# w2's gradient computed transposed, with the hidden activations as the moving side

## The chip, the cores and the metric

The kernel runs on one core of one Trainium2 chip. The metric is the device time of one execution in microseconds. A core has five engines that work side by side and wait for each other through semaphores: PE (matmuls), DVE (elementwise work and reductions), ACT (activations and copies), POOL, and SP, which here only issues transfers. SP, ACT and POOL each issue DMA transfers into a queue of their own; a transfer can be a plain copy or a DMA transpose of 2-byte elements. A matmul takes a stationary side (`lhsT`, 128 rows by up to 128 columns, loaded by a separate weight load) and a moving side (`rhs`, up to 512 columns here) and adds into PSUM, which has eight banks of 512 fp32 columns per partition.

## What is computed

One transformer block (a pre-LayerNorm linear attention with 32 heads, then a pre-LayerNorm SwiGLU MLP), forward and backward, in bf16: S = 2048 rows, D = 640, F = 1728.

```python
x = A_x
h = x + _A_ref(_layernorm(x), A_wqkv, A_wo)
h2 = h + _B_ref(_layernorm(h), B_w1, B_w3, B_w2)

def _B_ref(x, w1, w3, w2):
    gate = x @ w1                    # (2048, 640) @ (640, 1728)
    up = x @ w3
    h = silu(gate) * up              # called hh in the kernel
    return h @ w2                    # (2048, 1728) @ (1728, 640)

_out, _vjp = jax.vjp(_f, A_x, A_wqkv, A_wo, B_w1, B_w3, B_w2)
_grads = _vjp(grad_out)              # out_1 .. out_6
```

(The four matmuls are written here with `@`; the reference has them as einsums.) `out_6` is the gradient of w2: `hh.T @ grad_out`, 1728 rows by 640 columns, a sum over the 2048 rows of the sequence. It is the output that the change is about.

## The kernel before

All of it is one program, written out engine by engine in program order; each engine works its own instructions in that order. The stages, with their times in the profile:

- LayerNorm 1, the projections, the attention's sums (to about 107 us), and then attention output, LayerNorm 2 and the whole MLP forward with the elementwise half of its backward (to 341.8 us). It leaves `hh` transposed in DRAM as `hh_d` [F, S], and the gradients of gate and up as `gg_d` [2F, S].
- The w2 gradient (L1026 to L1096; 341.8 to 400.7 us), called *gw* here after its PSUM tile.
- The attention backward's first loop (L1242 to L1276; 400.7 to about 537 us), over the 16 tiles of 128 rows, `t` = 0 to 15.
- The rest of the attention backward (to 700.8 us), and at the end the gradients of w1 and w3 (L1538 to L1547; 700.8 to 817.4 us).

**gw before.** `load_hh(b)` brings a block of `hh_d` into SBUF by DMA transpose on SP's queue, as `hb[b]` [128, 16 row tiles, columns of F]. The blocks `blk` start at 0, 512, 1024 and 1536; the first is brought in two pieces of 256 columns so that PE can start on the first piece. `grad_out` lies in SBUF as `g2` [128, 16, 640]. For each 128 columns of F (`fc`, 13 of them) PE takes `hb` as the stationary and `g2` as the moving side, in two halves of 320 columns (`HD`), over 16 row tiles: 32 matmuls into two PSUM banks. ACT copies the two banks out (L1085) as one [128, 640] tile and stores it straight to `out_6` (L1086). The last 64 columns of F are `gw2_tail`: 32 matmuls of 64 stationary columns, the two halves of D in two halves of the array. While this runs, SP also loads what the next loop needs: w1 and w3 transposed (`load_w13`, into `w13a`, `w13b`) and the first two blocks of `gg_d` (`load_gg`, tiles `ggb`, two buffers, 256 rows of S each).

**The attention backward's first loop.** For tile t, PE does `ghn` (`b_ghn`, 54 matmuls of 320 columns: the gradient that comes back through the MLP to LayerNorm 2). ACT reads its PSUM tile (`gs`, L1139), DVE makes `wb`, ACT makes `y` (L1151) and DVE adds it into `g_h[:, t, :]`, the gradient of h (L1152). `b_gT(t)` then turns that tile on its side with a DMA transpose **on ACT's queue** (`ghT`, L1164, two buffers) for t < 14; the last two are turned on PE. PE uses it in `b_gr(t)` (`gr`, L1184, 10 matmuls), which stands in program order inside `b_ghn(t + 2)`, after four of its six groups of nine matmuls. DVE then makes `g_q[:, t, :]` from gr, the row tile `r_sb[:, t, :]` and others. Behind `ghT` on ACT's queue stands one more small DMA transpose for t = 1 to 10 (`woT`, then `kvN`, L1264), and at every even t from 2 on the second half of a `ggb` block (L1266). SP issues the first half of that `ggb` block, then `hnb` and `r_sb` for tile t + 2 (`b_load`), and from t = 4 on a tile of `xn_d` (`load_xn`), in this order; `hnb` has three buffers and so waits until `wb` of tile t - 1 is done.

**Order and waits.** Each transfer from SP or ACT counts up one of eight semaphores, given out in turn, and the builder lets a transfer wait until the one before it on the same semaphore has landed, so that eight are in flight at most. It adds waits for the data and, for DMA transposes, waits on transposes of the other queue. A waiting instruction holds everything behind it on its engine.

**The end.** The last loop (L1538) makes 35 products of up to 496 columns (`job`, `grad_job`), copies each out by ACT and stores it from ACT's queue; the first six are stored in two halves each.

Of the kernel before, what the change touches and what calls it, by code (L numbers as in the profile page):

```python
# [9 lines left out]
P = 128  # L10
BF16 = mybir.dt.bfloat16
F32 = mybir.dt.float32
# [6 lines left out]
S, D, H, F = 2048, 640, 32, 1728  # L19
DH = D // H  # L20
ST, DT = S // P, D // P
FT, FP = 14, 1792
FL = F - 13 * P
W, SC, TPC = 512, 4, 4
HD = D // 2
NG = 27
# [29 lines left out]
def kernel(  # L56
# [19 lines left out]
    V, A, T, G, SY = nc.vector, nc.scalar, nc.tensor, nc.gpsimd, nc.sync  # L76
    dma, dmaT, dmaG = SY.dma_start, SY.dma_start_transpose, G.dma_start
# [12 lines left out]
    dram = ctx.enter_context(tc.tile_pool(name="dram", bufs=1, space=bass.MemoryType.DRAM))  # L90
# [5 lines left out]
    w_d = dram.tile([D, D], BF16, name="w_d")  # L96
    kvT_d = dram.tile([D, D], BF16, name="kvT_d")
    dwoT_d = dram.tile([D, D], BF16, name="dwoT_d")
    hn_d = dram.tile([S, D], BF16, name="hn_d")
    hh_d = dram.tile([F, S], BF16, name="hh_d")  # L100
    gg_d = dram.tile([2 * F, S], BF16, name="gg_d")
# [2 lines left out]
    def pool(name, side="left", space=None):  # L104
        kw = dict(space=space) if space is not None else dict(side=side)
        return tc.alloc_tile_pool(name=name, bufs=1, reuse_waits="tile", **kw)
# [71 lines left out]
    ps = pool("p1p", space=PSUM)  # L178
# [48 lines left out]
    def load_w13(c0, c1):  # L227
        def go1():
            dma(out=w1[:, c0:c1, 0:F], in_=rows(B_w1)[:, c0:c1, :])

        def go3():
            dma(out=w3[:, c0:c1, :], in_=rows(B_w3)[:, c0:c1, 0:F - FL])
        return [go1, go3]
# [18 lines left out]
    def p1_tr(t, parts=((0, DT),)):  # L252
        xn = x_sb[:, t, :]
        for a, b in parts:
            tr = ps.tile([P, DT, P], BF16, name="tr", bufs=2)
            for c in range(a, b):
                T.transpose(tr[:, c, :], xn[:, c * P:(c + 1) * P], ident[:])

            A.copy(out=pqT[:, a:b, t * P:(t + 1) * P], in_=tr[:, a:b, :])  # L259
# [13 lines left out]
    def p1_mm(t, n0, between=None, halves=None):  # L273
        acc = p1_acc() if halves is None else None
        for j in range(2):
            p1_half(acc[:, j, 0:HD] if halves is None else halves[j][:, 0:HD], t, n0 + j * HD)
            if j == 0 and between is not None:
                between()
        return acc
# [241 lines left out]
    for t in range(ST):  # L521
        first = None
        if t < RAW:
# [11 lines left out]
            k = p1_mm(t, D, between, kh)  # L535
            act(0, 1)
            act(1, 1)
        else:
            k = p1_mm(t, D, (lambda: p1_tr(t + 1)) if t + 1 < XT_DMA else None)
# [95 lines left out]
    ps = pool("pap", space=PSUM)  # L635
# [342 lines left out]
    for c in range(SC):  # L978
# [9 lines left out]
        for fc in range(FT):  # L988
# [8 lines left out]
            if c == 0 and fc in (5, 7, 9, 11):  # L997
                a, b = {5: (0, 3), 7: (3, 6), 9: (6, 10), 11: (10, 13)}[fc]
# [10 lines left out]
            if c == SC - 1 and fc == 0:  # L1009
                g2 = U1.tile([P, ST, D], BF16, name="g2", tag="Q")  # L1010
                tail = U2.tile([P, DT, P], BF16, name="w13tail", tag="g2T", bufs=2)
            if c == SC - 1 and fc in (1, 2, 5, 6):
                i = (1, 2, 5, 6).index(fc)
# [9 lines left out]
    drain(1)  # L1023


    hb, blk = {}, [(0, 512), (512, 512), (1024, 512), (1536, 192)]  # L1026

    def load_hh(b):
        f0, fw = blk[b]
        hb[b] = U2.tile([P, ST, 512], BF16, name="hb", tag="ABCA"[b])  # L1030
        for a, n in ((0, 2 * P), (2 * P, 2 * P)) if b == 0 else ((0, fw),):
            dmaT(out=hb[b][:, :, a:a + n], in_=hh_d[f0 + a:f0 + a + n, :])

    load_hh(0)
    for _ in o2_steps(SC - 1, A.dma_start):
# [7 lines left out]
    br = pool("br", "right")  # L1043
    ps = pool("pcp", space=PSUM)
# [12 lines left out]
    def load_gg(j, c0, c1, q=dma):  # L1057
        if c0 == 0:
            ggb[j] = ba.tile([P, NG, 2 * P], BF16, name="ggb", bufs=2)
        q(out=ggb[j][:, c0:c1, :],  # L1060
            in_=gg_d[c0 * P:c1 * P, j * 2 * P:(j + 1) * 2 * P].rearrange("(c p) w -> p c w", p=P))

    def gw2_tail():

        gt = ps.tile([P, 2, 512], F32, name="gt", tag="gw", bufs=4)
        for t in range(ST):
            for j in range(2):
                T.matmul(gt[j * FL:(j + 1) * FL, 0, 0:HD], lhsT=hb[3][:, t, P:P + FL],
                         rhs=g2[:, t, j * HD:(j + 1) * HD], start=(t == 0), stop=(t == ST - 1))
        ob = br.tile([P, HD], BF16, name="gts")  # L1070
        A.copy(out=ob[:], in_=gt[:, 0, 0:HD])
        for j in range(2):
            A.dma_start(out=out_6[F - FL:F, j * HD:(j + 1) * HD], in_=ob[j * FL:(j + 1) * FL, :])

    for fc in range(FT - 1):
        b, i = divmod(fc, 4)
        if fc == FT - 2:
            gw2_tail()
        acc = ps.tile([P, 2, 512], F32, name="gw", bufs=4)
        for j in range(2):  # L1080
            for t in range(ST):
                T.matmul(acc[:, j, 0:HD], lhsT=hb[b][:, t, i * P:(i + 1) * P], rhs=g2[:, t, j * HD:(j + 1) * HD],  # L1082
                         start=(t == 0), stop=(t == ST - 1))
        ob = br.tile([P, D], BF16, name="gw2o", bufs=2)
        A.copy(out=ob[:].rearrange("p (j n) -> p j n", j=2), in_=acc[:, :, 0:HD])  # L1085
        A.dma_start(out=out_6[fc * P:(fc + 1) * P, :], in_=ob[:])  # L1086
        if fc == 3:
            load_hh(3)
        if fc == 5:
            load_w13()  # L1090
        if fc == 8:
            load_gg(0, 0, NG)
        if fc == 11:
            load_gg(1, 0, NG)
    ps.release()
    U2.release()  # L1096

# [6 lines left out]
    g_q = bl.tile([P, ST, D], BF16, name="g_q")  # L1104
    bo = pool("bo")
    r_sb = bo.tile([P, ST, D], BF16, name="r_sb")
    ps = pool("pbp", space=PSUM)
# [6 lines left out]
    def b_load(t):  # L1114
        hnb[t] = br.tile([P, D], BF16, name="hnb", bufs=3)
        dma(out=hnb[t][:], in_=hn_v[:, t, :])
        dma(out=r_sb[:, t, :], in_=r_v[:, t, :])
# [40 lines left out]
    def by_dma(t):  # L1158
        return t < ST - 2
# [35 lines left out]
    def b_gq(t):  # L1195
        V.tensor_tensor(out=two(sz[t][:]), in0=gr.pop(t)[:, :, 0:HD], in1=two(sz[t][:]), op=ALU.add)
        V.tensor_tensor(out=g_q[:, t, :], in0=sz.pop(t)[:], in1=cc.pop(t)[:], op=ALU.mult)
# [30 lines left out]
    def load_xn(a, b):  # L1228
        dma(out=xnN[:, a:b, :], in_=xn_v[:, a:b, :])
# [3 lines left out]
    def load_xnT(c):  # L1233
# [3 lines left out]
            xnT[c], xnT[c + 1] = both[:, 0], both[:, 1]  # L1237
        dmaT(out=xnT[c], in_=xn_d[c * W:(c + 1) * W, :])

    b_load(0)  # L1240
    b_load(1)
    for t in range(ST):  # L1242
        g = b_ghn(t)

        def part():
            next(g, None)

        u = t - 2
        ahead = 2 <= t <= ST - 4 and t % 2 == 0
        if ahead:  # L1250
            load_gg(t // 2 + 1, 0, FT)
        part()
        part()
        part()
        if t + 2 < ST:
            b_load(t + 2)
        if t >= 1:
            ln_rest.pop(t - 1)()
            if by_dma(t - 1):
                b_gT(t - 1)  # L1260
            if t <= 2 * DT:
                n = (t - 1) % DT
                dst, src = (woT, A_wo) if t <= DT else (kvN, kvT_d)
                A.dma_start_transpose(out=dst[:, :, n * P:(n + 1) * P], in_=src[n * P:(n + 1) * P, :])  # L1264
            if ahead:
                load_gg(t // 2 + 1, FT, NG, A.dma_start)  # L1266
        part()
        if u >= 0:
            b_gr(u)
        part()  # L1270
        part()
        if u >= 0:
            b_gq(u)

        if t >= 4:
            load_xn(t - 4, t - 3)  # L1276


    tri = U1.tile([P, 2 * DT, D], BF16, name="tri", tag="S0")
# [7 lines left out]
    a, b = ST - 1, ST - 2  # L1287
# [66 lines left out]
    ps = pool("pdp", space=PSUM)  # L1354
# [3 lines left out]
    def d_acc():  # L1358
        return ps.tile([P, 2, 512], F32, name="dkv", bufs=3)
# [20 lines left out]
    for m, (a, b) in enumerate(M_H):  # L1380
        n = (b - a) * DH
        acc = ps.tile([P, 512], F32, name="gkvT", tag="dkv", bufs=3)
        for c in range(DT):
            T.matmul(acc[:, 0:n], lhsT=woT[:, c, m * P:(m + 1) * P], rhs=QT[:, c, a * DH:b * DH], start=(c == 0),
                     stop=(c == DT - 1))
# [38 lines left out]
    acc = d_acc()  # L1424
    for m in range(DT):
        T.matmul(acc[:, m // 4, m % 4 * P:(m % 4 + 1) * P], lhsT=ones[:], rhs=gzd[:, m, :], start=(m % 4 == 0),
                 stop=True, skip_group_check=True)
# [3 lines left out]
    for t in range(ST):  # L1431
        c, i = divmod(t, TPC)
        u = t // 2
        acc = d_acc()
        for j in range(2):
            for k in range(DT):
                T.matmul(acc[:, j, 0:HD], lhsT=xnT[c][:, k, i * P:(i + 1) * P], rhs=gm[:, k, j * HD:(j + 1) * HD],  # L1437
                         start=(k == 0), stop=(k == DT - 1))
# [7 lines left out]
        if t in (2, 5, 8, 11, 14):  # L1446
            n = t // 3
            acc = square(mN, gkv_b, n)
            k = (4, 0, 1, 2, 3)[n]
            ob = obs[:, k * D:(k + 1) * D]  # L1450
# [6 lines left out]
        if t in (6, 8, 10, 12):  # L1457
            n = t // 2 - 3
# [48 lines left out]
    ps = pool("pep", space=PSUM)  # L1507
# [26 lines left out]
    ps = pool("pfp", space=PSUM)  # L1534
# [3 lines left out]
    for i, (f0, f1) in enumerate(blocks):  # L1538
        n = f1 - f0
        for m in range(DT):  # L1540
            last = (i, m) == (len(blocks) - 1, DT - 1)
            for a, b in ((0, n - P), (n - P, n)) if last else ((0, n),):
                c = (a + b) // 2
                halves = ((a, c), (c, b)) if i * DT + m < 6 else ((a, b),)
                out = [(x + y - a, z + y - a, to) for y, w in halves for x, z, to in both_grads(m, f0 + y, f0 + w)]
                grad_job(hnN, m, lambda t: gb[i][:, t, a:b], b - a, out, A.dma_start)
        load_block(i + 2)  # L1547
# [36 lines left out]
```

## Time and profile before

| | us |
|---|---|
| median of 3 runs | 821.91 (821.35 to 822.22) |
| the profiled execution, its time | 822.18 |
| its span, first to last instruction | 820.4 |
| PE busy | 812.7 (99% of the span) |
| ACT busy | 325.3 (40%) |
| DVE busy | 453.0 (55%) |
| gw, 416 matmuls of 320 columns, sum of the rows | 56.8 |
| gw's stretch 341.8 to 400.7 us: DMA share, GB/s | 1.20, 273 |
| the loop's stretch 419 to 467 us: DMA share, GB/s | 0.85, 193 |
| granted TensorE clock, in these stretches | 1.00 |

An instruction's row in the time line is: start (us from the span's start), length, engine, line, operation, output and inputs, shape; in brackets the idle time before it and what ended it. An engine's name with a q is its sequencer, as for an issued transfer; the transfer itself lands later, and "to landing" is the time from its issue until its semaphore counts up. PE's rows are matmuls in a pipeline: a row's own length (299 ns for 320 columns) is longer than the distance to the next (about 136 ns), and the distance is what adds up. The share of the DMA engines can read over 1 where two transfers overlap in one engine.

### The profile page before, as it was taken

The numbers are of one execution on the slowest core, as the hardware profiler recorded it, in microseconds if no ns is written. First come the engines' busy times: TensorE is split into PE (matmuls) and PEld (weight loads), VectorE is DVE, ScalarE is ACT, GpSimd is POOL, SyncE is SP. The second block draws the span as 40 slices with busy tenths as digits, with TensorE's granted clock in tenths as the row PEclk, the third lists the DMA queues.
The fourth block names the chain that finished last, engine by engine and source line by source line (L and its number), as shares of the span: only waits on it lengthen the run. The fifth ranks groups of instructions, "written<-read, shape, count | busy, mean of one in ns | idle before, by whom it ended". The sixth has DMA issues, their size and how long they took to land.

```text
span 820.4 us, 14028 instructions
## 1 busy us (share of the span) xinstructions
PE 812.7 (99%) x5437; PEld 512.9 (63%) x5464; DVE 453.0 (55%) x976; ACT 325.3 (40%) x605; POOL 131.0 (16%) x193
## 2 busy tenths in 40 slices
PE   8999999999999999999999999999999999999998
PEld 6677544555555545777777777777777777544444
DVE  7859887999898566300057777772781544200000
ACT  7856788655565666011122212222212334211111
POOL 2233333323322212100001111110220000000000
PEclk9999999999999999999999999999999999999999
DMA  9999989696485556999777897359996898978761
GB/s 231 252 271 237 210 233 321 191 240 156 140 218 156 159 188 167 223 263 257 220 173 178 207 204 187 72 113 180 240 210 125 166 197 158 238 166 191 167 138 37
DMA packets 322690, 157.57 MB, mean 192 GB/s; under 512 B 241728, under 2 KB 315872, under 8 KB 322624
## 3 DMA queue, kind: packets, MB, share of 16 engines
q1 hardware_dynamic: 279712, 115.85, 63.5%
q10 hardware_dynamic: 35584, 16.34, 9.3%
q0 software_dynamic: 7328, 24.48, 8.9%
q8 instruction: 43, 0.70, 0.4%
q14 instruction: 23, 0.19, 0.1%
HBM read 47.09 MB, written 51.13 MB: 120 GB/s over the span
## 4 chain that ended last, share of the span: by engine, by line
PE 95%; DMA 3%; DVE 1%; ACT 1%; issue 0%; SPq 0%; DVEq 0%
PE mm L387 20%; PE job L1331 20%; PE ghn L1127 14%; PE gxn L1500 8%; PE gw L1082 7%; PE o L895 4%; PE o L841 3%; PE big L267 3%; PE gwo L1215 3%; PE gr L1184 3%; PE dkv L1437 3%; PE macc L422 2%; PE at L648 2%; PE mm L267 1%; DMA pqT<-pql 1%; DMA wqkv<-in_A_wqkv_dram 1%
## 5 line engine op out<-in xcount | busy, mean ns | idle before, releaser
L1331 PE MATMUL job<-gb,hnN 128*128 128x496 bf16 (+3 forms) x576 | 116.8, 366 | 0.0
L1127 PEld LDWEIGHTS <-ggb 128*128 128x128 bf16 x864 | 84.5, 98 | 32.9
L1331 PEld LDWEIGHTS <-hnN 128*128 128x128 bf16 x576 | 55.7, 98 | 61.1
L387 PE MATMUL mm<-pqT,w 128*128 128x512 bf16 x397 | 93.2, 379 | 0.5
L387 PEld LDWEIGHTS <-w 128*128 128x128 bf16 x540 | 52.5, 98 | 63.1 <-issue 1.1
L1335 ACT CAST obs<-job 128x496 bf16<-128x496 f32 (+4 forms) x56 | 28.5, 509 | 123.7 <-PE job L1331 123.7
L1127 PE MATMUL ghn<-w13a,ggb 128*128 128x320 bf16 x448 | 63.5, 299 | 0.0
L1142 DVE SCALAR_TENSOR_TENSOR wb<-gs,hnb 128x640 f32<-128x640 bf16 x16 | 13.2, 826 | 89.8 <-ACT gs L1139 89.8
L1127 PE MATMUL ghn<-w13b,ggb 128*128 128x320 bf16 x416 | 61.4, 299 | 0.0
L387 PE MATMUL mm<-g2T,w2T 128*128 128x512 bf16 x227 | 58.5, 379 | 0.6
L1082 PE MATMUL gw<-g,hb 128*128 128x320 bf16 x416 | 56.8, 299 | 0.0
L1192 POOL TENSOR_TENSOR sz<-Zb,g_h 128x640 f32<-128x640 bf16 x16 | 20.2, 1260 | 197.7 <-DVE g_h L1193 197.7
L1082 PEld LDWEIGHTS <-hb 128*128 128x128 bf16 x416 | 40.6, 98 | 16.0 <-issue 0.3
L412 ACT CAST ghh<-mm 128x512 bf16<-128x512 f32 x48 | 28.3, 589 | 43.5 <-PE mm L387 36.8
L778 ACT ACTIVATE sig<-mm 128x512 bf16<-128x512 f32 x56 | 33.7, 602 | 25.7 <-PE mm L387 22.0
L1139 ACT ACTIVATE gs<-ghn 128x640 bf16<-128x640 f32 x16 | 11.2, 703 | 78.8 <-PE ghn L1127 58.4
L387 PEld LDWEIGHTS <-w2T 128*128 128x128 bf16 x260 | 25.3, 98 | 23.3
L267 PEld LDWEIGHTS <-pqT 128*128 128x128 bf16 x320 | 30.4, 98 | 14.2 <-ACT pqT L259 0.9
L267 PE MATMUL big<-wqkv,pqT 128*128 128x320 bf16 x250 | 38.4, 299 | 0.5 <-DMA pqT<-x_sb 0.3
L1331 PEld LDWEIGHTS <-g 128*128 128x128 bf16 x320 | 31.0, 98 | 11.6
L814 DVE TENSOR_TENSOR gate<-gate,sig 128x1024 bf16<-128x1024 bf16 x28 | 19.3, 690 | 33.7 <-ACT gate L789 33.6
L789 ACT CAST gate<-mm 128x512 bf16<-128x512 f32 x56 | 33.6, 600 | 4.1 <-DMA gg_d<-gate 4.0
(216 smaller groups left out, 1372.7 us busy)
## 6 DMA issues: line engine op xcount, KB each, us to landing
hh_d<-hhT SPq DMA_DIRECT2D x24, 256.0 KB, 2.8
gg_d<-gate POOLq DMA_DIRECT2D x24, 256.0 KB, 4.6
gg_d<-ghh POOLq DMA_DIRECT2D x24, 256.0 KB, 3.9
ggb<-gg_d SPq DMA_DIRECT2D x6, 896.0 KB, 5.3
ggb<-gg_d ACTq DMA_DIRECT2D x6, 832.0 KB, 5.7
x_sb<-in_A_x_dram SPq DMA_DIRECT2D x6, 640.0 KB, 5.7
ggb<-gg_d SPq DMA_DIRECT2D x2, 1728.0 KB, 12.7
pk_d<-pk_all SPq DMA_DIRECT2D x4, 640.0 KB, 8.0
```

The source lines that it names most:

```text
L267: T.matmul(acc, lhsT=pqT[:, c, t * P:(t + 1) * P], rhs=wqkv[:, c, n0:n0 + HD], start=(c == 0), stop=(c == DT - 1))
L387: T.matmul(acc[:], lhsT=w[:, c, fc * P:(fc + 1) * P], rhs=rhs[:, c, :], start=(c == 0), stop=(c == DT - 1))
L412: A.copy(out=ghh[n // 2][:, n % 2, :], in_=acc[:])
L778: A.activation(sig[:, i, :], gp[:], AF.Sigmoid)
L789: A.copy(out=gate[:, i, :], in_=gp[:])
L841: T.matmul(accs[i, j][:, 0:HD], lhsT=hhT[c][:, fc, i * P:(i + 1) * P], rhs=w2[:, fc, j * HD:(j + 1) * HD], start=(first and fc == 0), stop ...
L895: T.matmul(o2["ps"][:, 0:HD], lhsT=hhT[c][:, fc, i * P:(i + 1) * P], rhs=w2[:, fc, j * HD:(j + 1) * HD], start=(fc == 0), stop=(fc == FT - 1))
L1082: T.matmul(acc[:, j, 0:HD], lhsT=hb[b][:, t, i * P:(i + 1) * P], rhs=g2[:, t, j * HD:(j + 1) * HD], start=(t == 0), stop=(t == ST - 1))
L1127: T.matmul(acc[:, j, 0:HD], lhsT=ggb[t // 2][:, k, lo:lo + P], rhs=rhs[:, j * HD:(j + 1) * HD], start=(k == 0), stop=(k == NG - 1))
L1331: T.matmul(acc[:, 0:n], lhsT=lhs[:, t, m * P:(m + 1) * P], rhs=rhs(t), start=(t == 0), stop=(t == ST - 1))
L1335: A.copy(out=ob, in_=acc[:, 0:n])
L1500: T.matmul(acc[:, j, 0:HD], lhsT=g, rhs=wqT[:, k, j * HD:(j + 1) * HD], start=(k == 0), stop=(k == 14))
```

## The change

The w2 gradient is computed as its transpose, `grad_out.T @ hh`, 640 rows by 1728 columns: `g2` becomes the stationary side (128 of the 640 columns, `m` = 0 to 4) and `hb` the moving side, whole blocks of up to 512 columns. The blocks are now 256, 512, 512 and 448 columns, each brought by one DMA transpose; `gw2_tail` is gone. PSUM goes from four tiles of two banks to eight of one. ACT copies each [128, up to 512] tile and stores it into a new DRAM tile `gw2T_d` [640, 1728], on ACT's queue: 20 stores in place of 15. `load_hh(3)`, `load_w13` and the two `load_gg` come after blocks 0, 1, 2 and 3.

In the attention backward `gw2_turn(b)` reads block b of `gw2T_d` back with a DMA transpose on SP's queue, into rows 12 to 15 of `g_q` or `r_sb`, which have no content yet at that time, and `gw2_out(b)` stores it from there to `out_6`, one tile later. The turns stand at t = 2 to 5, the stores at t = 3 to 6, at the end of the tile in SP's order, stores first. Block 3 is turned in two pieces, 384 and 64 columns of F; in the built program the small one is no DMA transpose but a plain copy of 64 x 640 single elements (2 bytes each, 3,456 bytes apart in `gw2T_d`). In the last loop the first eight jobs' outputs are stored in halves, where it was six.

```diff
+    gw2T_d = dram.tile([D, F], BF16, name="gw2T_d")
...
-    hb, blk = {}, [(0, 512), (512, 512), (1024, 512), (1536, 192)]
+    hb, blk = {}, [(0, 256), (256, 512), (768, 512), (1280, 448)]
...
-        for a, n in ((0, 2 * P), (2 * P, 2 * P)) if b == 0 else ((0, fw),):
-            dmaT(out=hb[b][:, :, a:a + n], in_=hh_d[f0 + a:f0 + a + n, :])
+        dmaT(out=hb[b][:, :, 0:fw], in_=hh_d[f0:f0 + fw, :])
...
-    for fc in range(FT - 1):
-        b, i = divmod(fc, 4)
-        if fc == FT - 2:
-            gw2_tail()
-        acc = ps.tile([P, 2, 512], F32, name="gw", bufs=4)
-        for j in range(2):
+    for b, (f0, fw) in enumerate(blk):
+        for m in range(DT):
+            acc = ps.tile([P, 512], F32, name="gw", bufs=8)
             for t in range(ST):
-                T.matmul(acc[:, j, 0:HD], lhsT=hb[b][:, t, i * P:(i + 1) * P], rhs=g2[:, t, j * HD:(j + 1) * HD],
-                         start=(t == 0), stop=(t == ST - 1))
-        ob = br.tile([P, D], BF16, name="gw2o", bufs=2)
-        A.copy(out=ob[:].rearrange("p (j n) -> p j n", j=2), in_=acc[:, :, 0:HD])
-        A.dma_start(out=out_6[fc * P:(fc + 1) * P, :], in_=ob[:])
-        if fc == 3:
+                T.matmul(acc[:, 0:fw], lhsT=g2[:, t, m * P:(m + 1) * P], rhs=hb[b][:, t, 0:fw], start=(t == 0),
+                         stop=(t == ST - 1))
+            ob = br.tile([P, 512], BF16, name="gw2o", bufs=3)
+            A.copy(out=ob[:, 0:fw], in_=acc[:, 0:fw])
+            A.dma_start(out=gw2T_d[m * P:(m + 1) * P, f0:f0 + fw], in_=ob[:, 0:fw])
+        if b == 0:
             load_hh(3)
-        if fc == 5:
+        if b == 1:
             load_w13()
-        if fc == 8:
-            load_gg(0, 0, NG)
-        if fc == 11:
-            load_gg(1, 0, NG)
+        if b > 1:
+            load_gg(b - 2, 0, NG)
...
+    def gw2_turn(b):
+        f0, fw = blk[b]
+        dst = (g_q, r_sb)[b % 2]
+        n = fw // P
+        dmaT(out=dst[:, 12:12 + n, :], in_=gw2T_d[:, f0:f0 + n * P])
+        if fw % P:
+            dmaT(out=dst[0:fw % P, 12 + n, :], in_=gw2T_d[:, f0 + n * P:f0 + fw])
+
+    def gw2_out(b):
+        f0, fw = blk[b]
+        src, n = (g_q, r_sb)[b % 2], fw // P
+        dma(out=out_6[f0:f0 + n * P, :].rearrange("(k p) d -> p k d", p=P), in_=src[:, 12:12 + n, :])
+        if fw % P:
+            dma(out=out_6[f0 + n * P:f0 + fw, :], in_=src[0:fw % P, 12 + n, :])
...
         if t >= 4:
             load_xn(t - 4, t - 3)
+        if 3 <= t < 7:
+            gw2_out(t - 3)
+        if 2 <= t < 6:
+            gw2_turn(t - 2)
...
-                halves = ((a, c), (c, b)) if i * DT + m < 6 else ((a, b),)
+                halves = ((a, c), (c, b)) if i * DT + m < 8 else ((a, b),)
```

More of the change, by code (lines that the diff above doesn't have):

```diff
@@ L1061, in load_gg @@
             in_=gg_d[c0 * P:c1 * P, j * 2 * P:(j + 1) * 2 * P].rearrange("(c p) w -> p c w", p=P))
-    def gw2_tail():
-        gt = ps.tile([P, 2, 512], F32, name="gt", tag="gw", bufs=4)
-        for t in range(ST):
-            for j in range(2):
[L1068 to L1073, printed above, removed]
-    for fc in range(FT - 1):
-        b, i = divmod(fc, 4)
-        if fc == FT - 2:
-            gw2_tail()
-        acc = ps.tile([P, 2, 512], F32, name="gw", bufs=4)
-        for j in range(2):
-            for t in range(ST):
-                T.matmul(acc[:, j, 0:HD], lhsT=hb[b][:, t, i * P:(i + 1) * P], rhs=g2[:, t, j * HD:(j + 1) * HD],
-                         start=(t == 0), stop=(t == ST - 1))
-        ob = br.tile([P, D], BF16, name="gw2o", bufs=2)
-        A.copy(out=ob[:].rearrange("p (j n) -> p j n", j=2), in_=acc[:, :, 0:HD])
-        A.dma_start(out=out_6[fc * P:(fc + 1) * P, :], in_=ob[:])
-        if fc == 3:
+    for b, (f0, fw) in enumerate(blk):
+        for m in range(DT):
+            acc = ps.tile([P, 512], F32, name="gw", bufs=8)
+            for t in range(ST):
+                T.matmul(acc[:, 0:fw], lhsT=g2[:, t, m * P:(m + 1) * P], rhs=hb[b][:, t, 0:fw], start=(t == 0),
[4 more added lines that the diff above has]
+        if b == 0:
             load_hh(3)
-        if fc == 5:
+        if b == 1:
             load_w13()
-        if fc == 8:
-            load_gg(0, 0, NG)
-        if fc == 11:
-            load_gg(1, 0, NG)
+        if b > 1:
+            load_gg(b - 2, 0, NG)
     ps.release()
```

## The prediction

> **What bounds the kernel now.** I read the chain of waits first, then ACT's time line, then the landing times of transfers.
>
> ```profile
> PE 95%; DMA 3%; DVE 1%; ACT 1%; issue 0%; SPq 0%; DVEq 0%
> ...
> 396.28 4.45 PE gw L1082 x32
> 400.73 19.56 PE ghn L1127 x144
> 420.29 1.36 PE gr L1184 x10
> 421.65 7.33 PE ghn L1127 x54
> 428.99 1.36 PE gr L1184 x10
> 430.35 7.33 PE ghn L1127 x54
> 437.68 1.36 PE gr L1184 x10
> ```
>
> The first line is the page's chain by engine, the rest the chain in order of time (start, length, what). PE sets the end: from 300 to 817 us the chain is PE's but for some 0.2 us of issue. So only shorter PE work or a new wait of PE counts. In the attention backward a tile `t` takes 8.69 us (7.33 of ghn, 1.36 of gr). gr(t-2) stands inside ghn(t), so PE reads `ghT` at 428.99 (tile 1), 437.68 (2), 446.37 (3), 455.07 (4), 463.76 (5), and starts ghn(8) at 467.4. How early does ghT come?
>
> ```profile
> 418.30 0.92 ACT L1151 ACTIVATE y<-wb,s,ln_rs 128x640 bf16<-128x640 f32 x1 [2.07 <-DVE wb L1147]
> 419.78 1.22 ACTq L1164 DMA_TRANSPOSE ghT<-g_h  x1
> 421.04 1.30 ACTq L1264 DMA_TRANSPOSE woT<-in_A_wo_dram  x1
> 422.53 0.87 ACTq L1060 DMA_DIRECT2D ggb<-gg_d  x1
> 424.13 0.70 ACT L1139 ACTIVATE gs<-ghn 128x640 bf16<-128x640 f32 x1 [4.91 <-DMA ghT<-g_h]
> ```
>
> ACT's rows of one tile, issues included: ghT(1) issues at 419.78 and lands 4.6 us later (other tiles 2.6 to 4.6), at 424.4; PE wants it at 428.99. 4.6 us in hand, the same in each tile. Behind ghT on ACT stand woT, a ggb load and the next tile's gs.
>
> **PE's own work.** A matmul costs a + b x columns. 54 of 320 columns take 7.33 us, 135.7 ns each; the last stage's 576 take 116.65 us on the chain, 202.5 ns at 480 columns on average; so b = 0.417 and a = 2.4 ns. Removed: 416 x 135.8 = 56.5 us and gw2_tail's 32 in 2.29, 58.8. Added: 80 each of 256, 512, 512 and 448 columns, 80 x (109.1 + 215.7 + 215.7 + 189.1 ns) = 58.4. **PE gains 0.4 us.**
>
> **The load of hb.** hb[0] issues and lands as before (330.81, 341.4). hb[1] is now 512 wide and issues at 336.2. Before, the next 256 columns landed at 345.55 and 512 more at 353.70, so it should land at 341.4 + 4.2 + 8.15/2 = 349.6. Block 0 is short, 8.7 us, and ends at 350.55: 0.9 in hand, cost 0. At the third load's pace (512 columns in 10.7 us) PE waits 1.5; a gain is excluded, hb[0] being unchanged.
>
> **ACT and stores** in that stage: 0. 20 copies of about 0.6 us stand against 13 of 0.69, and ACT idles 55.9 us waiting for gw. Some stores now wait in ACT's queue for an older w13 or ggb transfer, up to 7 us; eight PSUM banks of 3.45 us matmuls cover it, and if they ran out PE would wait the rest. w13 and ggb move the same bytes. The last stage's two more split stores, 0.4 us of issue each, lie in ACT's 123.7 us of idling there.
>
> **The turns as transposes.** What ties them to ACT, the built program's list of waits shows: ghT(1) waits for turn 0 to land, ghT(2) for turn 1, ghT(4) for turn 2, ghT(5) for turn 3; turn 2 waits for ghT(3) and woT(4), turn 3 for ghT(4) and woT(5). ACT stands still meanwhile.
>
> The Trainium skill, "DMA: Bandwidth & Descriptors", section "Silent corruption: two transposing streams in flight at once", demands such waits, which speaks against this change; no run here shows the corruption. By the rule each turn ahead of a ghT is paid in full; without it they would share bandwidth.
>
> Price of a turn, from the same 640 KB elsewhere (median us to landing):
>
> ```profile
> ghT<-g_h ACTq DMA_TRANSPOSE x14, 3.5
> ...
> w2T<-in_B_w_dram SPq DMA_TRANSPOSE x5, 6.1
> ...
> g2T<-in_grad_out_dram SPq DMA_TRANSPOSE x4, 8.9
> ...
> xnT<-xn_d SPq DMA_TRANSPOSE x4, 5.6
> ```
>
> xnT spans 4.9 to 8.0, g2T 5.8 to 10.1. DMA's share is 0.85 from 419 to 467: I take 6.5 for 512 columns (4.9 to 9), 4.8 for 256 (the least w2T; 3.4, between ghT's 2.6 and xnT's 4.9, to 5.4), 5.0 for 384 (4.2 to 7), and 4.5 for a ghT beside other loads. gs to y is 2.86 us, y to ghT 1.94, ghT 1.24 and woT 1.30 on ACT.
> - Turn 0: SP is free at 419.1; lands 423.9. ghT(1) lands 428.4 for 428.99: 0. gs(2) slips from 424.13 to 427.3.
> - Turn 1: issues at 431.4, behind hnb, r_sb and a store; lands 437.9. ghT(2) lands 442.4 for 437.68: **4.7**.
> - gs(3) starts at 440.4, ghT(3) at 445.2, in time. woT(4) lands at 450.5, turn 2 at 457.0, ghT(4) at 461.5 for 455.07 + 4.7: **1.7**.
> - woT(5) lands at 461.1, turn 3 at 466.1, ghT(5) at 470.6 for 463.76 + 6.4: **0.4**.
>
> Sum 6.8 (with the least prices 1.8, with the greatest 15.6).
>
> **The turn's last piece.** Block 3 leaves 64 columns. The built program turns them with no transpose: a plain copy, 64 x 640 single elements of 2 bytes, 3,456 bytes apart in DRAM. 40,960 elements on 16 DMA engines are 2,560 each. Nothing in the trace moves single elements. Its packets, by size: 4 bytes (semaphore writes) 9 ns, 128 bytes 13, 256 bytes (what transposes move) 18, 512 bytes 27. Bounds: 2,560 x 9 = 23 us and x 27 = 69 us; less is excluded by the 4-byte row. I take 18 ns, since transposes' packets too jump from row to row: **46 us**, from 466.1 to 512.2.
>
> The skill says in the same page, "Rules for kernel authors", that a strided last dimension becomes one descriptor per element, and gives 19 times for such a copy against the transpose. From ghT's estimated 1 us of transfer per 160 KB, half of it times 19 would be some 10 us and the sum 837; no row here shows it.
>
> Who stands behind it on SP? The first half of ggb[4], then hnb, r_sb and xn of tile 6. SP's queue is first in, first out: an hnb behind two ggb blocks at 390.34 landed 12.0 us after its issue, others in 2.2 to 3.5. That half moves 112 packets per engine at 30 ns, 3.4 us, and lands at 515.6. ghn(8) wants it at 467.4 + 6.8 = 474.2. The built program also lets ACT's half of ggb[4] wait for it (a shared semaphore), and gs(6) stands behind that, which frees the PSUM tile that ghn(8) needs: start at 517.4, a wait of 43.2. gs(6) so late puts ghT(6) about 1.8 behind gr(6). **45.0 us.** After that the order runs free: out stores, hnb and r_sb land together, and a tile's chain needs about 9 of the 13.6 us it has.
>
> The granted clock reads 1.00 in every stretch; PE never idles over 1.1 us. The skill's "TensorE: Matmul & The Clock Gate", section "What's actually happening", halves the clock after about 3.4 us idle: an estimated 1.7 us more per long wait.
>
> The profiled execution took 822.18 us (span 820.4): 822.18 - 0.4 + 6.8 + 45.0 = 873.6; on the median of 821.91, **873**.
>
> **Rivals.** (1) **All is covered**, not slower: no ghT and no ggb is late, 821.5. For it: 4.6 us per ghT, and ggb is asked for 17 us ahead. Against: turn 1 cannot start before 430, and ghT(2) would have to issue by 433.2. It decides if turns take about 4 us and the piece under 5. (2) **The piece is short**, elements gathered in fewer packets: 2 to 15 us, so only the transposes' waits and a little of ggb, 828 to 842. Against: each element is a DRAM row of its own. (3) **The piece is dear**, 36 ns or more per element (twice a transpose's packet): 92 us, 828.6 + 92 - 1.1 = 919 or more. For it: no packet here is so scattered. (4) hb[1] late adds 1.5 to any.
>
> **How the numbers follow.** Forecast (9 to 27 ns, 850 to 896): 0.62. Short piece: 0.14. Dear: 0.17. Covered: 0.07. The range 838 to 920 leaves out the last, most of the second and part of the third. Within 0.2%, 1.6 us, a measurement cannot tell it from no change: same 0.05, faster 0.02, both out of the covered case; slower 0.93.
>
> **What would show it.** gw from 58.9 to 58.5 us; short waits of PE for ghT before gr(2) and gr(4); one long wait before ghn(8), ended by ggb, while SP's queue moves 2-byte packets. Wrong, if ghn(8) follows ghn(7) at once, if PE waits for hb, or if tiles 2 to 7 keep 8.69 us.

## The result, and the profile after

| | us |
|---|---|
| before, median of 6 runs | 822.07 (821.35 to 823.78) |
| changed, median of 6 runs | 889.86 (888.68 to 894.65) |
| ratio | 1.0833, 95% interval 1.0820 to 1.0846: slower |
| changed, the profiled execution and its span | 894.65, 892.9 |

The profiled execution is the longest of the six; the sums below are made against its span, 892.9 - 820.4 = 72.5 us more than before.

The page of the changed kernel, first the slices of PE's busy share and of the granted clock, then the chain by engine:

```profile
PE   9999999999999999999796027999999999999998
...
PEclk9999999999999999999987658999999999999999
...
PE 80%; DMA 7%; another core or an unknown queue 6%; DVE 3%; ACTq 1%; ACT 1%; SPq 1%; issue 1%; POOL 0%; DVEq 0%
```

Before, PE held 95% of the chain and the clock read 1.00 in every stretch that I had looked at. Now there is a hole (slices of 22.3 us, so at 424 to 558 us) and the clock is down in it. The "unknown queue" is where the chain's reading lost the thread, as its rows show (start, length, what):

```profile
402.48 0.54 ACT gw2o L1070
403.07 16.52 PE ghn L1110 x108
...
436.13 5.74 DMA r_sb<-gw2T_d
441.95 1.22 ACTq L1147
...
475.49 53.55 another core or an unknown queue
529.49 0.80 ACT gs L1122 x2
...
534.28 8.09 DMA ghT<-g_h
542.41 2.85 PE gr L1167 x10
```

Where before only PE's rows stood, the chain now goes from ACT's last gw2o copy to ghn(0), from a turn to a ghT's issue, and from gs(6) by ghT(6) to gr(6). What lies in the 53.55 us is told by the time lines of SP and ACT (start, length, engine, line; for an issue the length includes the time it is held up):

```profile
470.04 0.72 SPq L1229 DMA_DIRECT2D r_sb<-gw2T_d  x1
470.86 50.30 SPq L1060 DMA_DIRECT2D ggb<-gg_d  x1
```

```profile
529.06 0.38 ACTq L1060 DMA_DIRECT2D ggb<-gg_d  x1
529.49 0.70 ACT L1122 ACTIVATE gs<-ghn 128x640 bf16<-128x640 f32 x1 [60.10 <-DMA ggb<-gg_d]
```

The copy of single elements issues at 470.04 and lands at 526.19. The ggb half right behind it takes 50.30 us to be put into SP's queue and lands at 529.04; 0.02 us later ACT issues its half, which had waited for that one, and then gs(6). That is the chain of the prediction, event by event. It also shows what lengthens the kernel: between 419.6 and 542.4 us no row of PE stands in the chain, so of what PE loses in that stretch nothing adds to the time by itself; the turns, the copy, the ggb half and the steps of ACT and DVE between them set the pace.

PE's waits (who, what ended it: us in total, times, longest), with no such wait in the loop before:

```profile
PE ghn L1110 <- ACT gs L1122: 39.8, 1, 39.8
PE gr L1167 <- DMA ghT<-g_h: 14.3, 3, 8.3
PE gr L1167 <- DVE s L1127: 4.6, 1, 4.6
PE ghn L1110 <- ACT gw2o L1070: 2.5, 1, 2.5
```

One by one, from PE's time line: ghn(0) 2.50, gr(2) 4.58 (the page names DVE's `s`; its ghT landed at 446.38, PE went on at 446.43), gr(4) 0.53, gr(5) 8.29, ghn(8) 39.76, gr(6) 5.49. Sum 61.2. The rest is PE's pace after the waits:

```profile
403.07 5.64 PE L1110 MATMUL ghn<-w13a,ggb 128*128 128x320 bf16 x28 [2.50 <-ACT gw2o L1070]
...
419.41 3.97 PE L1110 MATMUL ghn<-w13a,ggb 128*128 128x320 bf16 x28
...
424.30 1.52 PE L1167 MATMUL gr<-wT,ghT 128*128 128x320 bf16 x10
...
484.18 2.85 PE L1167 MATMUL gr<-wT,ghT 128*128 128x320 bf16 x10 [8.29 <-DMA ghT<-g_h]
...
530.33 5.51 PE L1110 MATMUL ghn<-w13a,ggb 128*128 128x320 bf16 x28 [39.76 <-ACT gs L1122]
```

The same 28 matmuls take 3.97 us, and 5.64 or 5.51 after a wait; the same 10 of gr 1.52, and 2.85 after one. Over the rows behind each wait the loss is 1.67 (ghn(0)), 2.57 (gr(2)), 2.47 (gr(5)), 1.54 (ghn(8)) and 2.37 (gr(6)), 10.6 us in all. As an account of PE's time, 61.2 + 10.6 = 71.8 of the 72.5; the gw stage gives 0.34 back and starts 0.34 later; the remaining 0.7 I have not traced. The granted clock reads 0.50 in these places and 1.00 between them, for 3.4 us from 403.8 on and 6.8 us from 444.8 and from 540.3 on, among others.

The landing times that answer to the table of before (median us, last column):

```profile
ghT<-g_h ACTq DMA_TRANSPOSE x14, 3.9
...
r_sb<-gw2T_d SPq DMA_DIRECT2D x1, 80.0 KB, 56.2
...
g_q<-gw2T_d SPq DMA_TRANSPOSE x2, 5.3
...
r_sb<-gw2T_d SPq DMA_TRANSPOSE x2, 5.5
```

The second row is the copy of single elements.

### The profile page after: what moved, and what is told of

It reads as the page before. It is cut to its first block, busy times and chain, and to the rows that moved or that the text cites. A ratio compares the mean times of both kernels' runs of the same rounds, so it can differ in the third digit from the quotient of the medians.

```text
span 892.9 us, 13804 instructions
## 1 busy us (share of the span) xinstructions
PE 824.1 (92%) x5305; PEld 506.1 (57%) x5336; DVE 452.4 (51%) x976; ACT 325.8 (36%) x611; POOL 131.1 (15%) x193
## 3 DMA queue, kind: packets, MB, share of 16 engines
HBM read 47.17 MB, written 53.35 MB: 113 GB/s over the span
## 4 chain that ended last, share of the span: by engine, by line
PE 80%; DMA 7%; another core or an unknown queue 6%; DVE 3%; ACTq 1%; ACT 1%; SPq 1%; issue 1%; POOL 0%; DVEq 0%
PE mm L388 19%; PE job L1333 18%; PE ghn L1110 8%; PE gxn L1502 7%; PE gw L1067 4%; PE big L268 4%; PE o L896 3%; PE o L842 3%; PE gwo L1198 3%; PE macc L423 2%; PE dkv L1439 2%; PE at L649 2%; PE gr L1167 2%; DMA g_q<-gw2T_d 1%; DMA ggb<-gg_d 1%
## 5 line engine op out<-in xcount | busy, mean ns | idle before, releaser
L1110 PEld LDWEIGHTS <-ggb 128*128 128x128 bf16 x864 | 87.4, 101 | 80.0 <-DMA ggb<-gg_d 38.8
L1110 PE MATMUL ghn<-w13a,ggb 128*128 128x320 bf16 x448 | 66.7, 309 | 42.3 <-ACT gs L1122 39.8
L1110 PE MATMUL ghn<-w13b,ggb 128*128 128x320 bf16 x416 | 64.8, 310 | 0.0
L1067 PE MATMUL gw<-hb,g 128*128 128x512 bf16 (+2 forms) x316 | 58.4, 345 | 0.2
L1067 PEld LDWEIGHTS <-g 128*128 128x128 bf16 x320 | 31.3, 98 | 27.0
L1167 PE MATMUL gr<-wT,ghT 128*128 128x320 bf16 x160 | 28.3, 331 | 18.9 <-DMA ghT<-g_h 14.3
L1333 PEld LDWEIGHTS <-g 128*128 128x128 bf16 x320 | 31.0, 98 | 11.6
## 6 DMA issues: line engine op xcount, KB each, us to landing
ggb<-gg_d SPq DMA_DIRECT2D x2, 1728.0 KB, 11.9
```

The costliest lines, as they stand in the source:

```text
L1067: T.matmul(acc[:, 0:fw], lhsT=g2[:, t, m * P:(m + 1) * P], rhs=hb[b][:, t, 0:fw], start=(t == 0), stop=(t == ST - 1))
L1110: T.matmul(acc[:, j, 0:HD], lhsT=ggb[t // 2][:, k, lo:lo + P], rhs=rhs[:, j * HD:(j + 1) * HD], start=(k == 0), stop=(k == NG - 1))
L1167: T.matmul(gr[t][:, j, 0:HD], lhsT=ghT[t][:, c, :], rhs=wT2[:, c, j * HD:(j + 1) * HD], start=(c == 0), stop=(c == DT - 1))
L1333: T.matmul(acc[:, 0:n], lhsT=lhs[:, t, m * P:(m + 1) * P], rhs=rhs(t), start=(t == 0), stop=(t == ST - 1))
```

## The experiments

The first four are the changed kernel with one thing altered; before ran beside them at a median of 822.58 (821.92 to 824.03). The others are small programs of their own, which compute nothing of the block but repeat one part of it; their total time says nothing.

### Without the element copy

```diff
-            dmaT(out=dst[0:fw % P, 12 + n, :], in_=gw2T_d[:, f0 + n * P:f0 + fw])
+            dmaT(out=dst[:, 12 + n, :], in_=gw2T_d[:, F - P:F])
...
-            dma(out=out_6[f0 + n * P:f0 + fw, :], in_=src[0:fw % P, 12 + n, :])
+            dma(out=out_6[f0 + n * P:f0 + fw, :], in_=src[P - fw % P:P, 12 + n, :])
```

> The last 64 columns are turned by a true DMA transpose of the last 128 columns of F (64 of them turned twice); no element copy is left. If the element copy is what costs (it holds 53 us of SP's queue), what stays is the 2.5 us of ghn(0), 4.6 of gr(2), 0.5 of gr(4), 1 to 4 of gr(5) and some 4 us of lower clock: 832 to 838 us, and no wait before ghn(8). If the turns' transposes and their waits across the two queues are the main cost, it stays above 860.

Measured: 846.69 us (842.93 to 850.18), ratio 1.0289, interval 1.0255 to 1.0324. PE's waits in this kernel's profile (842.93 us):

```profile
PE gr L1167 <- DMA ghT<-g_h: 6.4, 1, 6.4
PE gr L1167 <- DVE s L1128: 5.0, 1, 5.0
PE ghn L1110 <- ACT gw2o L1070: 2.3, 1, 2.3
PE gr L1167 <- DVE wb L1125: 1.8, 1, 1.8
```

ghn(8) waits for nothing any more. So the element copy is worth 889.86 - 846.69 = 43 of the 68 us, net of the small transpose that replaces it. But the rest is 24 us, not the 10 to 16 I expected. The profiled run, the fastest of the four, is 20.7 above before: 15.5 of waits, and 4.6 of slower pace after two of them. The largest wait, 6.4 before gr(5), is a pile-up that I had not worked out: the last turn lands at 473.51, and only then ghT(5) issues, beside a ggb half, hnb and r_sb that had stood behind the turns on SP; it takes 8.2 us. After the wait of 2.31 us PE's pace is full, unlike in the changed kernel after 2.50:

```profile
403.18 3.96 PE L1110 MATMUL ghn<-w13a,ggb 128*128 128x320 bf16 x28 [2.31 <-ACT gw2o L1070]
```

### The same elements, spread

```diff
+        if 6 <= t < 14:
+            e = (t - 6) * 80
+            dmaT(out=g_q[0:FL, 15, e:e + 80], in_=gw2T_d[e:e + 80, F - FL:F])
+        if t == 15:
+            dma(out=out_6[F - FL:F, :], in_=g_q[0:FL, 15, :])
```

> The same 40,960 single elements are copied, but in eight copies of 5,120 elements, one per tile at t = 6 to 13, at the end of the tile in SP's order, into another tile; stored at t = 15. At 20.9 ns per element and engine each takes 6.7 us. If the cost is the queue's order (a 53 us transfer with ggb[4] behind it), the long wait vanishes and 833 to 851 us remain, the upper end if each ghT beside such a copy comes some 2 us late. If the cost is the load of single elements on the DMA engines, wherever it stands, the 53 us come back in pieces: 880 to 895.

Measured: 876.77 us (874.91 to 878.76), ratio 1.0656, interval 1.0635 to 1.0678. Only 13 us came back; the time lies between the two ranges that I had expected. The wait before ghn(8) is 0.7, as the queue's order says, but PE now waits for eight ghT, the last five of them (24.2 us) from the first small copy on:

```profile
PE gr L1167 <- DMA ghT<-g_h: 34.9, 8, 9.3
```

Its chain of waits tells why:

```profile
500.78 16.21 DMA g_q<-gw2T_d
517.07 1.22 ACTq L1147
...
526.08 17.08 DMA g_q<-gw2T_d
543.23 1.22 ACTq L1147
```

Each small copy takes 10 to 17 us from issue to landing (6.7 expected), and five ghT issue within 0.1 us of a copy's landing. ghT uses no data of it; its issue waits for the semaphore that the copy was the last to count up, which is the semaphore that this ghT counts up next. The median ghT, once issued, takes 7.6 us for 3.5 before. So a copy of single elements costs in three ways: what stands behind it in its queue, what draws the same semaphore on either queue, and what moves beside it. My theory held the first alone to matter, and fell here.

### No turn at all

```diff
+    o6T = out_6[:, :].rearrange("f d -> (f d)").rearrange("(d f) -> d f", f=F)
...
-            A.dma_start(out=gw2T_d[m * P:(m + 1) * P, f0:f0 + fw], in_=ob[:, 0:fw])
+            A.dma_start(out=o6T[m * P:(m + 1) * P, f0:f0 + fw], in_=ob[:, 0:fw])
...
-        if 3 <= t < 7:
-            gw2_out(t - 3)
-        if 2 <= t < 6:
-            gw2_turn(t - 2)
```

> The gradient is computed transposed and stored, in the transpose's order, straight into out_6's memory; no turn and no store of a turned block is left, so the turning of the output is left out. What the gw stage itself does to the time: PE's matmuls 0.4 us shorter, ghn(0) waits 2.5 us for ACT's last copies, and a lower clock after it: 823 to 826. If that wait is covered or belongs to the turns: 821.5 to 822.

Measured: 829.72 us (828.35 to 830.90), ratio 1.0083, interval 1.0067 to 1.0100. In the loop no wait is left, all 8.69 us tiles. Most of the loss is one wait and the slow pace behind it (the first 144 matmuls of ghn take 21.94 us for 19.72), 7.9 of the 8.7 us that the profiled run is above before; 0.5 more is a wait of PE for hb[0] in this run:

```profile
PE ghn L1111 <- ACT gw2o L1071: 5.6, 1, 5.6
```

So the gw stage costs by itself, in the changed kernel 2.5 + 1.7 us. The changed kernel's ACT time line shows how (in brackets idle time and what ended it):

```profile
392.79 0.53 ACT L1070 CAST gw2o<-gw 128x448 bf16<-128x448 f32 x1 [3.74 <-DMA gw2T_d<-gw2o]
395.33 0.34 ACTq L1071 DMA_DIRECT2D gw2T_d<-gw2o  x1
...
401.49 0.53 ACT L1070 CAST gw2o<-gw 128x448 bf16<-128x448 f32 x1 [4.19 <-DMA gw2T_d<-gw2o]
402.05 0.34 ACTq L1071 DMA_DIRECT2D gw2T_d<-gw2o  x1
402.48 0.53 ACT L1070 CAST gw2o<-gw 128x448 bf16<-128x448 f32 x1 [0.47 <-ACT gw2o L1070]
```

Block 3's first store stands from 393.3 to 395.33, until 0.08 us after ggb[0] lands (395.25): the same semaphore, by the trace. Everything behind it on ACT slips, the fourth copy waits for a gw2o buffer, and the last copy ends at 403.0, when PE has been through with gw for 2.5 us. In the kernel without turns the two ggb loads landed 4 us later (399.23 and 405.46), and the wait was longer by 3. The turns come after these loads, so that is not their doing; where it comes from is not shown, and the 7 us of this run are more than the stage costs in the changed kernel.

### Keeping PE busy through the long wait

```diff
-        n = 0
+        n = -324 if t == 7 else 0
...
-        for k in range(NG):
+        for k in [*range(NG)] * (7 if t == 7 else 1):
...
-                if n % 9 == 0 and n < 54:
+                if n % 9 == 0 and 0 < n < 54:
```

> The changed kernel with ghn(7) computed seven times over (324 matmuls more, 44 us at 135.7 ns, same result), ahead of the two long waits of PE (8.3 and 39.8 us). The waits then shrink to about 4 us in all. If the idle PE runs at a lower clock afterwards, as the granted clock of 0.66 from 470 to 540 us suggests, the clock stays up and the kernel is 5 to 9 us faster than the changed one in spite of 44 us more work: 881 to 885. If the lower clock has another cause (the DMA load, the queue), the time stays at 889 to 895.

Measured: 895.81 us (893.14 to 901.60), ratio 1.0906, interval 1.0858 to 1.0954: not faster than the changed kernel, so the expectation of the clock theory failed. The clock did stay higher (0.87 from 500 to 540 us for 0.58), but PE's waits before ghn(8) and gr(6) were still 9.9 and 2.6 us, not about 4 in all:

```profile
PE ghn L1110 <- ACT gs L1122: 9.9, 1, 9.9
```

But a PE that is ready earlier only waits for the same landing: ggb's half came at 532.40, and from there the end is 360.1 us away, for 363.9 in the changed kernel. The faster pace is worth these 3.8 us at most (1.9 of them a ghT that landed sooner). After the wait of 2.63 us before gr(6) no pace was lost, its 10 matmuls took 1.53 us; after the 9.85 us before ghn(8) 2.5 were. The element copy landed 59.5 us after its issue for 56.2. Why it took longer, and why the median is some 6 us up, stays open.

### What a single element costs

One program of copies; `far` has the shape and the row distance of the copy in question, `ggs` the shape of half a ggb block:

```python
col = B_w1[:, F - FL:F].rearrange("d f -> f d")
def far(q, a, b):
    q(out=el[0:FL, a:b].unsqueeze(2), in_=col[:, a:b].unsqueeze(2))
...
far(dma, 0, D); far(dma, 0, 2 * P); far(dma, 0, D)
dma(out=el[:, 0:D:2].unsqueeze(2), in_=B_w1[0:P, 0:HD].unsqueeze(2))
dma(out=el[0:FL, 0:2 * D:2].unsqueeze(2), in_=B_w1[0:FL, 0:D].unsqueeze(2))
...
far(dma, 0, D)
dma(out=sp2[:], in_=ggs)
...
A.dma_start(out=ac2[:], in_=ggs)
for i in range(10):
    A.dma_start(out=sm[i][:], in_=xS[:, i, :])
```

> Only copies, nothing of the block is computed. From the last 64 columns of w1 (as far apart in DRAM as those of gw2T_d, 3,456 bytes): 64 x 640 single elements, 64 x 256, 64 x 640 again; then two copies of 40,960 single elements read from neighbouring places; then the same 80 KB as 640 rows of 128 bytes, one row tile, two ggb-like loads; each alone. Last, 64 x 640 elements on SP with a ggb-like load behind it on SP, one on ACT beside it, and ten row tiles on ACT. If the price is one per element (some 20.9 ns per element and DMA engine): 53, 21, 53, 53, 53 us. If it is the jump between rows of DRAM, the two from neighbouring places take under 25 us. If the copy holds only its own queue, SP's load lands some 5 us after it and ACT's load beside it takes at most twice its time alone; the row tile on ACT whose semaphore was last used by the copy issues only once the copy has landed. If the load on the DMA engines decides, ACT's load beside it takes most of the 53 us too.

Measured, alone and one after the other: 53.37, 22.6 (to the next issue), 53.28 us; from neighbouring places 35.04 (128 x 320) and 53.33 (64 x 640); the same 80 KB as 640 rows of 128 bytes 2.12 us. 53.3 us over 2,560 elements per DMA engine are 20.8 ns each. Distance in DRAM is not what costs: neighbours 2 bytes apart took the same 53.33 us. Then beside and behind it (name, engine, count, KB each, median us to landing):

```profile
gg<-in_grad_out_dram SPq DMA_DIRECT2D x2, 896.0 KB, 5.8
...
sp<-in_grad_out_dram SPq DMA_DIRECT2D x1, 896.0 KB, 59.1
ac<-in_grad_out_dram ACTq DMA_DIRECT2D x1, 896.0 KB, 9.1
el<-in_B_w_dram SPq DMA_DIRECT2D x6, 80.0 KB, 53.3
```

A load that takes 5.8 us alone takes 9.1 beside the element copy on the other queue, and 59.1 behind it on the same one, landing 2.85 us after it. And of ACT's ten row tiles the fourth, next on the copy's semaphore, issued at 289.86, the copy having landed at 289.83: ACT stood some 52 us (from 238.2 on) for a transfer of SP's. These are the three ways of the spread run, told apart.

### Which shape of element copy

```python
for p, n, st in ((P, HD, 1), (FL, D, 1), (FL // 2, 2 * D, 1), (P, HD, 2)):
    src = (B_w1 if n <= D else B_w2)[0:n, 0:p]
    dma(out=el[0:p, 0:n * st:st].unsqueeze(2), in_=src.rearrange("d f -> f d").unsqueeze(2))
```

> Four copies of 40,960 single elements alone, to tell what made one of the copies of neighbouring elements cheaper (35 us for 53): 128 partitions x 320, 64 x 640, 32 x 1,280, all read from places 3,456 or 1,280 bytes apart and written densely, and 128 x 320 written to every second place. If the number of partitions sets it: 35, 53, 70 or more, 35 us. If it was that the elements were read from neighbours: 53 for all four. If the place written sets it, only the last takes 35.

Measured: 34.88, 53.53, 53.35, 34.02 us. Neither where the elements come from nor how densely they are written matters; over 128 partitions the same count takes 35 us, over 64 or 32 it takes 53. It is not in proportion to the partitions, so the expectation held for the first two and the last and missed the third. What makes the step between 128 and 64 stays open.

### PE's pace after idle gaps

```python
for n in (0, 1, 2, 4, 6, 8, 10, 12, 16, 24, 48):
    V.tensor_copy(out=z[:, 0:HD], in_=acc[:, 0:HD])
    for _ in range(n):
        V.tensor_scalar(out=z[:], in0=z[:], scalar1=1.0, scalar2=None, op0=ALU.mult)
    V.tensor_copy(out=b[:, 0:HD], in_=z[:, 0:HD])
    acc = mms(200)
```

> Nothing of the block is computed: groups of 200 matmuls of 320 columns with idle gaps of PE between them, growing from about 1 to about 40 us (DVE works on one tile in between). The changed kernel's rows show 1.7 us lost after an idle 2.5 us, 2.6 after 4.6, 2.4 after 8.3. If a fixed stretch of slow clock follows each gap over some 2 us, each long gap loses about 1.7 to 2.7 us, the longest no more than one of 5. If the loss grows with the gap, the longest loses several times as much.

Measured, PE's time line (start, length of 200 matmuls, in brackets the gap ahead of them):

```profile
59.57 27.33 PE L102 MATMUL acc<-b,a 128*128 128x320 bf16 x200 [1.47 <-DVE b L110]
88.89 29.00 PE L102 MATMUL acc<-b,a 128*128 128x320 bf16 x200 [2.00 <-DVE b L110]
120.95 30.20 PE L102 MATMUL acc<-b,a 128*128 128x320 bf16 x200 [3.06 <-DVE b L110]
...
399.72 29.07 PE L102 MATMUL acc<-b,a 128*128 128x320 bf16 x200 [26.29 <-DVE b L110]
```

Nothing is lost after 1.47 us; after 2.00 us and all longer gaps 1.4 to 2.9 us are, and 26.3 us lose no more (1.7) than 3.06 (2.9). It is a price per gap, and the changed kernel's 1.5 to 2.6 lie in it. After the 2.00 us the granted clock reads 0.50 from 89.3 to 92.7 us and 1.00 from there on: 3.4 us at half speed are the 1.7 lost. But the length of the gap alone does not decide: after 2.31 us (without the element copy) and 2.63 us (before gr(6), with PE kept busy) nothing was lost. Within a run the stretches at 0.50 begin and end on one raster of 3.41 us and last one, two or more of its steps, so where in the raster a gap falls may decide; no run tested that. The Trainium skill, "TensorE: Matmul & The Clock Gate", section "What's actually happening", puts the slow state after an idle window of about 3.4 us; here a gap of 2.00 us was enough, and the measurement decides.

### A model of the end of gw

The same 320 matmuls, copies and stores, plain loads of w13's size and the two ggb loads from SP, then four ghn. In the first pair of runs the loads fell as they did in the model, in the second pair 1.3 MB more stood ahead of ggb; in each pair one has block 3's stores on ACT, the other on POOL with five buffers:

```diff
-            ob = br.tile([P, 512], BF16, name="gw2o", bufs=3)
+            ob = br.tile([P, 512], BF16, name="gw2o", bufs=5)
...
-            (A if b < 3 else A).dma_start(out=gw2T_d[m * P:(m + 1) * P, f0:f0 + fw], in_=ob[:, 0:fw])
+            (A if b < 3 else G).dma_start(out=gw2T_d[m * P:(m + 1) * P, f0:f0 + fw], in_=ob[:, 0:fw])
```

> A model of the gw stage and of the tiles after it, without the rest of the block: the same 320 matmuls, copies and stores from ACT's queue, two loads of w13's size (plain) and the two ggb loads from SP's queue at the changed kernel's places, then four ghn. If ACT's stores stand behind ggb transfers (one of eight shared semaphores), one of block 3's stores issues only as a ggb load lands, and PE waits 1 to 6 us for gw2o before its first ghn, as in the changed kernel (2.5). If not, PE's first ghn waits for data alone or for nothing.

> The same model with block 3's five stores issued from POOL's queue and five gw2o buffers for three. If the shared semaphore is the cause, block 3's copies on ACT follow PE within a us and PE's wait for gw2o before the first ghn is gone. If it is the copies themselves or the data, the wait stays as it was.

Measured: a wait for gw2o of 0.6 us in both. The loads landed too early to hold ACT, so this pair tells nothing of the cause but the floor: PE's first ghn waits 0.6 us for the last copy in any case.

> The model of the gw stage again, with 1.3 MB more to load ahead of the two ggb loads, so that they land some 6 us later against PE, as they did in the changed kernel (there, the first landed 7 us after block 3's first product was ready). The shared semaphore as cause: block 3's first and fourth store on ACT issue within 0.1 us of the landing of ggb[0] and ggb[1], the copies behind them come late, and PE's wait before the first ghn grows from 0.6 to 2 us or more. If ACT is not held, it stays at 0.6.

> As the run before it, with block 3's five stores from POOL's queue and five gw2o buffers. The shared semaphore as cause: the copies follow PE, and the wait before the first ghn is 0.6 us again, but for data. If the loads themselves are late for ghn, the wait stays as in the run before it.

Measured: 1.6 us with ACT's stores, 0.6 with POOL's. ACT's time line of the former:

```profile
73.54 0.53 ACT L127 CAST gw2o<-gw 128x448 bf16<-128x448 f32 x1 [2.49 <-PE gw L124]
76.76 0.33 ACTq L128 DMA_DIRECT2D gw2T_d<-gw2o  x1
77.50 0.53 ACT L127 CAST gw2o<-gw 128x448 bf16<-128x448 f32 x1 [3.42 <-DMA ggb<-gg_d]
```

The fourth store stands from 74.07 to 76.76, ggb[1] having landed at 76.69, and the last copy comes late by it. Only this store was held, not the first too as I expected, so the wait is 1.6 and not over 2; but the mechanism is shown, and that another queue's store undoes it, in the model (the buffers were changed along with the queue, but no copy of the former run had waited for one). The held store counts up the semaphore that ggb[1] did. In the kernel itself this was not tried.

## Why the prediction was right, and where it was not

Slower was right, the place and the chain were right, 889.86 lies in the range of 838 to 920, and it is 17 above the 873. Term by term, the profiled execution (894.65, 21 above the 873.6 that was worked out for it) beside the prediction:

| term | predicted | measured |
|---|---|---|
| gw on PE | -0.4 | -0.34 (58.57 us from first matmul to last, 58.91 before) |
| hb[1] lands | 349.6, no wait | 350.21, no wait |
| ACT and stores in gw | 0 | 2.50 before ghn(0) |
| gr(2), gr(4) | 4.7, 1.7 | 4.58, 0.53 |
| gr(5) | 0.4 | 8.29 |
| element copy | 46 (18 ns an element) | 53.4 after turn 3 landed (20.9 ns) |
| ghn(8) and gr(6) behind it | 43.2 + 1.8 | 39.76 + 5.49 |
| lower clock | nothing by rows | 10.6 |

**What the 21 us are made of.** Since no PE row is in the chain from 419.6 to 542.4 us, the terms do not simply add: ghn(8) waits for the same landing however late PE comes, and what PE lost before it was taken out of that wait. What counts is when the copy could start, how long it took, and what followed. Turn 3 landed at 472.76 for 466.1, 6.7 us late; 4.2 of these were there at turn 0 (issued at 423.31 for 419.1), and they are the 2.50 of ghn(0) and the 1.67 of slower pace behind it. The copy took 7.4 more than the 46. From its landing to gr(6) it was 16.2 us, where 11.9 follow from the prediction's numbers, 4.3 more, mostly a ghT(6) of 8.09 us for 4.5. The slower pace after gr(6) cost 2.4. Together 20.8.

**The element copy** was the main term, and the mechanism was right: single elements, SP's queue, ggb[4] behind it, ACT's half held by the shared semaphore. Its price was 7 us too low; 18 ns was the packet of transposes, a single element takes 20.8 alone. The reason I gave, that each lies in another DRAM row, is wrong: neighbours cost the same. The Trainium skill's factor of 19 ("DMA: Bandwidth & Descriptors", "Rules for kernel authors") I had turned into 10 us by an estimated 1 us of transfer; the fault was that base, for which I gave no row. In the run without the copy a DMA transpose of twice as many columns landed in 3.85 us, a fourteenth of the copy's 53.4, by the element a twenty-eighth, so the factor is of the right size.

**gr(5)** is a step that failed: 4.5 us for "a ghT beside other loads" was too little for what SP issues right behind the last turn. ghT(5) issued at 472.86 and took 11.27 us beside the copy; behind the same turns without the copy it took 8.2, beside the loads that then followed, and the wait was still 6.4. It cost the kernel nothing here, since ghn(8)'s wait swallowed it; without the copy it was the largest loss. The two waits ahead of it came out as worked out, though the turns took 5.2 to 5.7 us whether they were of 256, 384 or 512 columns, where I had 4.8, 5.0 and 6.5; errors of both signs partly cancelled, and ghn(0)'s late start moved PE and the turns alike.

**ACT and the stores** is the other failed step. "Some stores now wait in ACT's queue" was seen, but I let eight PSUM banks cover it. They cover gw's own matmuls; ghn(0) wants banks that ACT has not yet emptied, and it is the first instruction that has nothing behind it to hide in. I had looked for a shortage within the stage, not at its last instruction.

**The clock** I priced at nothing since no row of before showed it, and gave 1.7 us per long wait only beside the sum. In the changed kernel every wait of PE from 2.5 us on cost 1.5 to 2.6 more of PE's time. The kernel's time is longer by less: by the chain only the 1.67 after ghn(0) and the 2.37 after gr(6) count, as the other three fell into waits for a landing. With PE kept busy through the longest wait, the gain was used up by the next landing in the same way.

**The rivals.** All covered: excluded by the ratio. A short piece (under 15 us): excluded, 53 us alone. A dear one (36 ns or more): excluded, 20.8. hb[1] late: it was not, by 0.5 us (landed 350.21, PE started on it at 350.74).

What stays open: whether turns on ACT's own queue, where no transpose would wait for the other queue's, would be free, and whether with that and block 3's stores on another queue the kernel would come out at or below 822. Neither was tried. No run here beat the kernel before, and the gain to be had from gw on PE is 0.34 us.

## What to carry to other kernels

A DMA transpose of a remainder, here 64 columns, may be built as a copy of single elements, at some 21 ns each on every DMA engine (here over 64 partitions): look into the built program for element sizes of 2 bytes, and turn a full block of 128 columns that overlaps the last one instead. When a slow transfer enters a queue, list three kinds of victims: what stands behind it, what is next on its semaphore on any queue, and what moves beside it; spreading it out largely changes which of them pays (13 of 43 us came back here). And price a wait of PE from about 2 us on with up to 3 us more than its length, unless another wait follows that swallows it: follow the chain, not the sum of waits.

## What the runs showed of the hardware that was not expected

- 40,960 single elements of 2 bytes take 53.3 to 53.5 us over 64 or 32 partitions, 34 to 35 us over 128, wherever they lie in DRAM and however densely they are written; 80 KB in rows of 128 bytes take 2.1 us.
- A DMA turn of 256 columns (320 KB) landed no sooner than one of 512: 5.33 for 5.35 and 5.74 us, in the loop with its other loads. No run had them alone.
- PE's clock fell to half after an idle gap of 2.00 us, not after 1.47; but not after gaps of 2.31 and 2.63 in two other runs. The loss does not grow with the gap (1.7 us after 26.3), and the stretches at half clock last 3.4 us or a multiple.
